# One stage of a fused RWKV and mixture-of-experts kernel: narrower loads of k, other places for the routing's work

## The chip, the cores and the metric

The kernel runs on one core of a Trainium2 chip. The metric is the device time of one execution in microseconds (us). Three runs of the kernel before gave 303.65, 304.31 and 305.09 us; the median is 304.31 us. A separate execution was profiled; it took 301.18 us.

The core has five engines, each with its own in-order queue: PE (TensorE) multiplies matrices into PSUM, DVE (VectorE), ACT (ScalarE) and POOL (GpSimd) work on tiles, and SP issues nearly all the DMAs. An instruction that waits holds everything behind it on its engine.

## The reference

Attention part, for 4 batches, 8 heads, 768 tokens and a head dimension of 48:

```
for t in range(768):
    cur     = einsum('bhd,bhe->bhde', u * k[t], v[t])
    y[:, :, t] = einsum('bhd,bhde->bhe', r[t], state + cur)
    state   = w[t][..., None] * state + einsum('bhd,bhe->bhde', k[t], v[t])
```

Its output is laid out as 3072 tokens of 384 values, x, which go through a mixture of 8 experts (hidden width 1024) with a skip test:

```
compute = x @ w_skip > 0            # the other tokens are copied
e       = argmax(x @ w_gate)        # one expert for each token
out     = x + softmax_weight[e] * (relu(x @ w1[e]) @ w2[e])
```

## The kernel before, in words

The first half of the program is the attention part, the second half the experts. The attention is cut into 24 chunks of 128 tokens: 4 batches of 6 chunks, the state starting from zero in each batch. A loop `for s in range(-2, n + 1)` writes the work out by hand in a software pipeline; the order in which it is written is the order of every engine's queue. In step s it

- issues the loads of chunk s+4 (three buffers `wrk`; each holds w, r and k side by side in 1545 words for each row) and of v,
- prepares chunk s+2: `prep_scan` (DVE: scan q over w; POOL: rk = r*k for the bonus), `prep_keys` (DVE: L290 takes 1/q at the chunk's first token, L292 multiplies it by `rowsk`, which is one in the 96 rows in use and zero in the others, and puts it into the word ahead of w; POOL: kq = k*q), `prep_reads` (DVE: scan rh over w and that word; POOL: rp = r*rh),
- works on chunk s+1: `scores` (PE, from kq and rp), `rows_of_keys` (PE transposes kq, ACT copies it to kt), two `mask`s (DVE), `bonus_sums` (PE, into psY) and `bonus` (DVE multiplies psY by v),
- finishes chunk s: `update` and `carry` (PE adds kt*v to the state, ACT scales it and copies it to sblk), `outputs` (PE adds masked scores times v, and state times rp, to psY), `evict` (ACT copies psY to xT) and `rows_out` (PE turns xT back into rows and makes the gate logits).

psY is one buffer: `bonus_sums(s+1)` writes it only after ACT's copy xT of chunk s. A `wrk` buffer of 128 rows holds 96 rows in use (16 to 111); the 16 rows on each side are loaded from the neighbouring chunks in the same DMA and are finite but meaningless; `rowsk` makes what depends on them zero.

Every 6 chunks a `router` runs over the logits. It is a generator; `drip()` at fixed places in the step runs it on by one or two pieces, so its small DVE instructions fall between those of the chunks. What it wants done on PE or ACT it puts into the list `held`, which `flush()` empties at two places in the step, and it goes on only when the list is empty. `ranks` are eight short products of which DVE needs the result (`pss`); `places` are the products with one-hot rows (`hot`), which put token numbers into a table. One-hot rows are made by `mark`, two for each step, by two ACT operations each (`dd`, then `hot`); eight of 24 are made by DVE. After the third group, `early()` (L525) multiplies a count `ohs` by ones on PE (L528, psC), and starts a gather of the first expert's tokens, for which PE waits at the end of the attention.

In 12 of the steps a slice of an expert's weights is split in two parts for exactness: ACT casts the upper part (L89), and POOL subtracts it from the raw weights for the lower part (L90), at the end of the step.

Of the kernel before, what the change touches and what calls it, by code (L numbers as in the profile page):

```python
# [21 lines left out]
P = 128  # L22
# [34 lines left out]
def rwkv_moe_kernel(ctx, tc, wrk, wrk0, vN, uP, wgs, wgp, w12, cst, out):  # L57
# [40 lines left out]

    def drain(g):
        for _ in g:  # L100
            pass
# [20 lines left out]
    with tc.tile_pool(name="att", bufs=2) as att, \  # L122
# [22 lines left out]
        def load_chunk(i):  # L145
            b, c = seq[i]
            rows = wrk.rearrange("b c g d n -> (b c g d) n")
            at = 2 * D * i
            t = wrk_sb[i % NBUF]
            vt = vt_sb[i % (NBUF + 1)]  # L150
            if i == 0:
                nc.sync.dma_start(t[KO:LO, :R_OFF], rows[:2 * D, :R_OFF])
                nc.sync.dma_start(t[KO:LO, R_OFF:V_OFF], rows[:2 * D, R_OFF:V_OFF])
                nc.scalar.dma_start(c_sb[:, :C_IOTA], cst[:, :C_IOTA])
                shifted(nc.scalar, u_sb, uP)
                for g in range(2):
                    load_vt(nc.scalar, vt, i, g)
                return
            if i < n - 1:
                nc.sync.dma_start(t, rows[at - KO:at - KO + P, :V_OFF])  # L160
            else:
                nc.sync.dma_start(t[KO:LO], rows[at:at + 2 * D, :V_OFF])
            for o in range(2):
                load_vt(nc.sync, vt, i, o)
# [46 lines left out]
        hd = scratch(NP).rearrange("p (a o) -> p a o", o=1)  # L211
# [8 lines left out]
        def clear_rk(eng, i):  # L220
            eng.memset(wrk_sb[i][:, R_OFF:], 0.0)

        def setup():
# [4 lines left out]
            nc.vector.memset(warm, 0.0)  # L228
            nc.gpsimd.memset(vt_sb[1], 0.0)
            load_chunk(1)  # L230
            load_v(0)
            nc.vector.memset(pss, 0.0)
# [4 lines left out]
            nc.vector.tensor_reduce(rowsk, ident[:, KO:LO], axis=AX, op=ALU.add)  # L237
            nc.scalar.activation(junk0, warm[:, 0:1], AF.Exp)
            for z in psa:
                nc.scalar.copy(z.rearrange("p a j -> p (a j)"), warm)  # L240
            nc.gpsimd.memset(vt_sb[2], 0.0)
# [44 lines left out]
        def prep_keys(i):  # L286
            wk = work[i]
            heads = wk["w"][:, 0:NP * CW].rearrange("p (a j) -> p a j", a=NP)
            at = heads[:, :, 0:1]
            nc.vector.reciprocal(hd if i > 0 else at, wk["q"][:, :, 0:1])  # L290
            if i > 0:
                nc.vector.tensor_scalar(at, hd, rowsk, None, op0=ALU.mult)  # L292
            kq = wk["kq"] = att.tile([P, NP, P], F32, tag="kq", name=f"kq{i}")
            nc.gpsimd.tensor_tensor(kq, wk["k"], wk["q"][:, :, 1:1 + P], op=ALU.mult)  # L294
# [111 lines left out]
        def router(i0, m):  # L406
# [67 lines left out]
            def mark(c):  # L474
                dd = att.tile([P, 2 * P], BF16, tag="dd", name=f"dd{i0}_{c}")
                hot = att.tile([P, 2 * P], BF16, tag="hot", name=f"hot{i0}_{c}", bufs=NC)
                nc.scalar.activation(dd, iota, AF.Square, bias=r1[:, c], scale=-1.0)
                nc.scalar.activation(hot, dd, AF.Relu, bias=rows1_, scale=-2.0)
                hots[c] = hot
# [107 lines left out]
        with tc.manual_schedule():  # L587
            setup()
            fill(FILL0)
            for s in range(-2, n + 1):  # L590
# [16 lines left out]
                if s == LATE:  # L607
                    nc.sync.dma_start(wgs_sb, wgs)
                if on(s - 1):
# [15 lines left out]
                flush()  # L625
                if on(s + 2):
                    prep_keys(s + 2)
                    drip(pace[0])
                    if s != -1:
                        prep_reads(s + 2)  # L630
                if s == -2:
# [7 lines left out]
                if on(s + 1):  # L639
                    scores(s + 1)  # L640
                    rows_of_keys(s + 1)
                    drip(2 * pace[0])
# [3 lines left out]
                    bonus_sums(s + 1)  # L646
# [23 lines left out]
                if 3 <= k < 9:  # L670
                    split_slice(0, 3 + k, nc.gpsimd)
                if 12 <= k < 18:
                    split_slice(1, k - 12, nc.gpsimd)
# [349 lines left out]
```

## Time and profile before

| what | value |
|---|---|
| median of three runs | 304.31 us |
| the profiled execution | 301.18 us |
| its span, first to last instruction | 299.4 us |
| PE busy | 275.0 us, 92% of the span |
| DVE busy | 223.8 us, 75% |
| ACT busy | 168.1 us, 56% |
| POOL busy | 138.6 us, 46% |
| DMA, mean | 216 GB/s, 64.62 MB |

The shares are means over two stages. In the attention (about the first 149 us) PE, DVE, ACT and POOL all work, each waiting for the others; in the experts PE is busy without a gap. In the timeline an instruction's duration can overlap the next one's start on PE, so the distance between starts is what a piece of work costs there. "Idle before" and the bracket behind a row name what ended the engine's wait.

### The profile page before, as it was taken

To read this page: it belongs to the slowest core of one execution; us is meant where nothing else is said; L and a number is where in the kernel's file an instruction comes from. 1 tells how busy PE (TensorE), PEld (TensorE's weight loads), DVE (VectorE), ACT (ScalarE), POOL (GpSimd) and SP (SyncE) were. 2 spreads that over 40 slices of the span, in tenths; PEclk is the share of its full clock that TensorE was granted. 3 is DMA by queue.
4 is the path that set the end of the run, shared out by engine and by line. 5 is a ranking of instruction groups with operands and counts; after the bars stand their busy time and mean duration, and the time that the engine had idled before them with its cause. 6 is when DMAs were issued, how large, how long until landed. Compare 5 with 4: busy or idle time off the path is not lost.

```text
span 299.4 us, 8963 instructions
## 1 busy us (share of the span) xinstructions
PE 275.0 (92%) x3581; PEld 247.8 (83%) x3581; DVE 223.8 (75%) x434; ACT 168.1 (56%) x470; POOL 138.6 (46%) x136
## 2 busy tenths in 40 slices
PE   6697998998889979879999999999999999999993
PEld 2476877777767867768798999999999999999993
DVE  7869999898989988986373788784958859496320
ACT  3265645779565986587432485581837649183310
POOL 4867765969975689776115761402011020201101
PEclk9999999999999999999999999999999999999999
DMA  7979999996799968865604798866265663620001
GB/s 217 246 198 311 349 352 371 309 303 194 240 332 297 333 187 285 219 210 180 209 28 114 231 373 308 274 207 234 71 231 208 210 251 129 237 107 26 9 2 41
DMA packets 26548, 64.62 MB, mean 216 GB/s; under 512 B 4886, under 2 KB 15930, under 8 KB 26496
## 3 DMA queue, kind: packets, MB, share of 16 engines
q1 hardware_dynamic: 23904, 58.14, 59.4%
q0 software_dynamic: 2048, 5.48, 5.5%
q8 instruction: 30, 0.49, 0.7%
q10 hardware_dynamic: 544, 0.33, 0.6%
q14 instruction: 22, 0.18, 0.2%
HBM read 56.88 MB, written 7.86 MB: 216 GB/s over the span
## 4 chain that ended last, share of the span: by engine, by line
issue 32%; PE 12%; DVE 7%; DMA 7%; POOL 6%; ACT 5%; POOLq 1%; SPq 0%; DVEq 0%
POOL out L745 5%; DMA r<-w 4%; PE psY L378 2%; PE psH L115 2%; PE psA L326 2%; PE psX L394 2%; DMA vt<-wrk 2%; PE psY L382 1%; DMA xg<-out,idr 1%; PE psY L345 1%; DVE w2l L90 1%; DVE psY L349 1%; DVE asb L332 1%; ACT xT L387 1%; PE psT L316 1%
## 5 line engine op out<-in xcount | busy, mean ns | idle before, releaser
L745 POOL DMA_INDIRECT out<-fin,ids x16 | 16.9, 1058 | 101.1 <-DVE fin L840 93.3
L814 ACT ACTIVATE hh<-psH 128x256 fp32r<-128x256 f32 x60 | 23.1, 384 | 55.2 <-PE psH L809 52.1
L809 PE MATMUL psH<-xTh,w1l 128*128 128x256 f32 x168 | 47.5, 283 | 0.0
L808 PE MATMUL psH<-xTl,w1h 128*128 128x256 f32 x168 | 47.5, 283 | 0.0
L807 PE MATMUL psH<-xTh,w1h 128*128 128x256 f32 x168 | 47.5, 283 | 0.0
L831 PE MATMUL psO<-w2h,hh 128*128 128x384 f32 x120 | 40.9, 341 | 0.0
L833 PE MATMUL psO<-w2h,hl 128*128 128x384 f32 x120 | 40.2, 335 | 0.0
L832 PE MATMUL psO<-w2l,hh 128*128 128x384 f32 x120 | 40.1, 334 | 0.0
L819 DVE SCALAR_TENSOR_TENSOR hl<-psH,hh 128x256 fp32r<-128x256 f32 x60 | 25.2, 420 | 12.3 <-ACT hh L814 12.0
L378 PE MATMUL psY<-asb,v 128*48 128x128 f32 x384 | 26.5, 276 | 8.4 <-DVE psY L349 8.4
L304 POOL TENSOR_TENSOR rp<-wrk,rh 128x512 f32<-128x512 f32 x23 | 27.2, 1182 | 12.5 <-DVE rh L299 7.6
L283 POOL TENSOR_TENSOR rk<-wrk 128x512 f32<-128x512 f32 x24 | 31.3, 1304 | 3.6 <-DMA wrk<-wrk 3.6
L332 DVE TENSOR_TENSOR asb<-psA,c_sb 128x512 f32<-128x512 f32 x48 | 30.5, 677 | 3.0 <-PE psA L326 2.8
L274 DVE TENSOR_TENSOR_SCAN q<-wrk,pss 128x520 f32<-128x520 f32 x24 | 29.3, 1222 | 4.5 <-DMA wrk<-wrk 4.4
L294 POOL TENSOR_TENSOR kq<-wrk,q 128x512 f32<-128x512 f32 x24 | 28.3, 1180 | 8.6 <-DVE q L274 4.7
L809 PEld LDWEIGHTS psH<-xTh,w1l 128*128 128x128 f32 x168 | 32.2, 192 | 0.0
L808 PEld LDWEIGHTS psH<-xTl,w1h 128*128 128x128 f32 x168 | 32.2, 192 | 0.0
L807 PEld LDWEIGHTS psH<-xTh,w1h 128*128 128x128 f32 x168 | 32.2, 191 | 0.0
L299 DVE TENSOR_TENSOR_SCAN rh<-wrk,pss 128x520 f32<-128x520 f32 x24 | 29.7, 1236 | 1.7
L89 ACT CAST w2h<-r 128x512 fp32r<-128x512 f32 x48 | 27.9, 625 | 2.0 <-DMA r<-w 2.0
L90 DVE TENSOR_TENSOR w2l<-r,w2h 128x512 fp32r<-128x512 f32 x42 | 27.8, 687 | 1.5 <-ACT w2h L89 0.5
L378 PEld LDWEIGHTS psY<-asb,v 128*48 128x48 f32 x384 | 20.4, 123 | 10.0 <-DVE psY L349 9.8
(149 smaller groups left out, 594.3 us busy)
## 6 DMA issues: line engine op xcount, KB each, us to landing
r<-w SPq DMA_DIRECT2D x48, 512.0 KB, 5.3
wrk<-wrk SPq DMA_DIRECT2D x22, 772.5 KB, 5.8
v<-vN SPq DMA_DIRECT2D x24, 192.0 KB, 5.2
out<-x SPq DMA_DIRECT2D x24, 192.0 KB, 4.6
vt<-wrk SPq DMA_DIRECT2D x46, 96.0 KB, 5.3
wrk<-wrk SPq DMA_DIRECT2D x1, 579.4 KB, 4.8
wrk<-wrk SPq DMA_DIRECT2D x1, 384.0 KB, 4.4
out<-fin,ids POOLq DMA_INDIRECT x16, 3.9
```

The costliest lines, as they stand in the source:

```text
L90: (eng or nc.vector).tensor_tensor(dst_l, src, dst_h.bitcast(F32), op=ALU.subtract)
L283: nc.gpsimd.tensor_tensor(work[i]["rk"].rearrange("p a j -> p (a j)"), t[:, R_OFF:K_OFF], t[:, K_OFF:V_OFF], op=ALU.mult)
L299: nc.vector.tensor_tensor_scan(rh.rearrange("p a j -> p (a j)"), wk["w"][:, 0:NP * CW], ones_at[:, :NP * CW], 1.0, op0=ALU.mult, op1=ALU.max)
L332: nc.vector.tensor_tensor(s, psa[g], tri.rearrange("p (o j) -> p o j", o=1).to_broadcast([P, NP, P]), op=ALU.mult)
L378: nc.tensor.matmul(y_at(a, g), v[:, 2 * a + g], wk["asb"][g][:, a], start=False, stop=True, skip_group_check=True)
L745: sc = nc.gpsimd.indirect_dma_start(out=out, out_offset=bass.IndirectOffsetOnAxis(ap=ids[:, s % 2, s // 2:s // 2 + 1], axis=0), in_=o, in_ ...
L807: nc.tensor.matmul(ps, w1h[:, o:o + P], xTh[:, kc], start=(kc == 0), stop=False)
L808: nc.tensor.matmul(ps, w1h[:, o:o + P], xTl[:, kc], start=False, stop=False)
L809: nc.tensor.matmul(ps, w1l[:, o:o + P], xTh[:, kc], start=False, stop=(kc == KC - 1))
L831: nc.tensor.matmul(pso, h[j, fc][0], w2h[:, o], start=(fc == 0), stop=False)
L832: nc.tensor.matmul(pso, h[j, fc][0], w2l[:, o], start=False, stop=False)
L833: nc.tensor.matmul(pso, h[j, fc][1], w2h[:, o], start=False, stop=(fc == FC - 1))
```

## The change

Five edits, all in the attention part.

1. w and r are loaded by 128 rows as before, k by its 96 rows in a DMA of its own. The rows of k beside them are cleared once for each of the three buffers at the start (POOL), so every product with k is zero there. L292, the scratch word `hd` and the making of `rowsk` at the start go; the reciprocal writes straight into `wrk`. `rowsk`, which a test at the end still uses, is loaded by three small DMAs in step 18.
2. `mark` makes a one-hot row by one POOL instruction in place of two on ACT.
3. The lower part of a weight slice (POOL) is written one step later, behind the next step's rp; ACT's cast stays.
4. The first `flush()` of a step moves from behind `outputs(s)` to behind `rows_of_keys(s+1)`.
5. `bonus_sums(s+1)` moves from behind the masks to directly behind `scores(s+1)`, ahead of the transposes.

The core of the diff:

```diff
+    def split_high(e, i):
...
+        nc.scalar.copy(hi, raw)
+        low_parts.append(lambda: nc.gpsimd.tensor_tensor(lo, raw, hi.bitcast(F32),
+                                                         op=ALU.subtract))
...
-            if i < n - 1:
-                nc.sync.dma_start(t, rows[at - KO:at - KO + P, :V_OFF])
-            else:
-                nc.sync.dma_start(t[KO:LO], rows[at:at + 2 * D, :V_OFF])
-            for o in range(2):
-                load_vt(nc.sync, vt, i, o)
+            to, at_ = (t[:, :K_OFF], at - KO) if i < n - 1 else (t[KO:LO, :K_OFF], at)
+            nc.sync.dma_start(to, rows[at_:at_ + to.shape[0], :K_OFF])
+            nc.sync.dma_start(t[KO:LO, K_OFF:], rows[at:at + 2 * D, K_OFF:V_OFF])
+            if i > 1:
+                for o in range(2):
+                    load_vt(nc.sync, vt, i, o)
...
-            eng.memset(wrk_sb[i][:, R_OFF:], 0.0)
+            eng.memset(wrk_sb[i][:, R_OFF if i == 0 else K_OFF:], 0.0)
...
+            clear_rk(nc.gpsimd, 1)
+            load_chunk(1)
             nc.gpsimd.memset(vt_sb[1], 0.0)
-            load_chunk(1)
             load_v(0)
+            for o in range(2):
+                load_vt(nc.sync, vt_sb[1], 1, o)
...
-            nc.vector.tensor_reduce(rowsk, ident[:, KO:LO], axis=AX, op=ALU.add)
...
+            clear_rk(nc.gpsimd, 2)
             nc.gpsimd.memset(vt_sb[2], 0.0)
...
-            at = heads[:, :, 0:1]
-            nc.vector.reciprocal(hd if i > 0 else at, wk["q"][:, :, 0:1])
-            if i > 0:
-                nc.vector.tensor_scalar(at, hd, rowsk, None, op0=ALU.mult)
+            nc.vector.reciprocal(heads[:, :, 0:1], wk["q"][:, :, 0:1])
...
             def mark(c):
-                dd = att.tile([P, 2 * P], BF16, tag="dd", name=f"dd{i0}_{c}")
                 hot = att.tile([P, 2 * P], BF16, tag="hot", name=f"hot{i0}_{c}", bufs=NC)
-                nc.scalar.activation(dd, iota, AF.Square, bias=r1[:, c], scale=-1.0)
-                nc.scalar.activation(hot, dd, AF.Relu, bias=rows1_, scale=-2.0)
+                nc.gpsimd.tensor_scalar(hot, iota, r1[:, c], None, op0=ALU.is_equal)
...
                 if s == LATE:
                     nc.sync.dma_start(wgs_sb, wgs)
+                    shifted(nc.sync, rowsk, cst[:, C_HS + 2:C_HS + 3])
...
                     outputs(s)
-                flush()
                 if on(s + 2):
                     prep_keys(s + 2)
                     drip(pace[0])
                     if s != -1:
                         prep_reads(s + 2)
+                while low_parts:
+                    low_parts.pop()()
...
                     scores(s + 1)
+                    bonus_sums(s + 1)
                     rows_of_keys(s + 1)
+                    flush()
                     drip(2 * pace[0])
                     mask(s + 1, 0)
                     mask(s + 1, 1)
                     drip(pace[0])
-                    bonus_sums(s + 1)
                     bonus(s + 1)
...
                 if 3 <= k < 9:
-                    split_slice(0, 3 + k, nc.gpsimd)
+                    split_high(0, 3 + k)
                 if 12 <= k < 18:
-                    split_slice(1, k - 12, nc.gpsimd)
+                    split_high(1, k - 12)
```

Three places show how the queues change. Line numbers of the new kernel are higher by 10 to 18 for the same instruction, and a scan is named SCALAR_TENSOR_TENSOR here.

DVE at the ranks of the first group, before; `oh` is what the ranks need, `pss<-ex` (the sum of the exponentials) lies in the PSUM bank that they write, `asb` are the masks:

```order
L274 SCALAR_TENSOR_TENSOR q_922<-wrk_86,pss 128x520
L432 TENSOR_TENSOR oh_926<-key,pss 128x48
L290 RECIPROCAL pss<-q_922 128x4
L292 TENSOR_SCALAR wrk_86<-pss,rowsk 128x4
L447 TENSOR_REDUCE pss<-ex_840 128x6
L299 SCALAR_TENSOR_TENSOR rh_956<-wrk_86,pss 128x520
L449 TENSOR_SCALAR pss<-pss 128x6
L452 RECIPROCAL gall<-pss 128x6
L332 TENSOR_TENSOR asb_8_988<-psA_111,c_sb 128x512
L332 TENSOR_TENSOR asb_8_990<-psA_112,c_sb 128x512
```

DVE at the same place in the changed kernel:

```order
L288 SCALAR_TENSOR_TENSOR q_925<-wrk_86,pss 128x520
L443 TENSOR_TENSOR oh_929<-key,pss 128x48
L303 RECIPROCAL wrk_86<-q_925 128x4
L310 SCALAR_TENSOR_TENSOR rh_950<-wrk_86,pss 128x520
L458 TENSOR_REDUCE pss<-ex_843 128x6
L460 TENSOR_SCALAR pss<-pss 128x6
L343 TENSOR_TENSOR asb_8_997<-psA_111,c_sb 128x512
L343 TENSOR_TENSOR asb_8_999<-psA_112,c_sb 128x512
```

L292 is gone, and the two small instructions on `pss` that stood around the scan rh now both stand between rh and the masks.

PE at the same place, before, from the last product of `outputs` (state times rp) to the ranks, which the scores of chunk 8 follow:

```order
L382 MATMUL psY<-rp_750,sblk_114 48x128 x8
L435 LDWEIGHTS trib
L435 MATMUL pss<-oh_926,trib 128x48
L437 LDWEIGHTS onesb
L437 MATMUL pss<-ohs,onesb 128x48
L440 LDWEIGHTS onesb
L440 MATMUL pss<-oh_926,onesb 128x40
```

PE there in the changed kernel, from the last product of the scores:

```order
L337 MATMUL psA_112<-rp_846,kq_840 64x64
L356 MATMUL psY<-rk_826,ubk_sb 48x128 x8
L327 MATMUL psT_981<-c_sb,kq_840 128x128 x4
L446 LDWEIGHTS trib
L446 MATMUL pss<-oh_929,trib 128x48
L448 LDWEIGHTS onesb
L448 MATMUL pss<-ohs,onesb 128x48
L451 LDWEIGHTS onesb
L451 MATMUL pss<-oh_929,onesb 128x40
L451 LDWEIGHTS onesb
```

The ranks stand behind the scores, the bonus sums (`psY<-rk`) and the transposes (`psT`) of chunk 8, no longer ahead of them.

POOL at the end of the third group, before, from the rp of chunk 22 to the first gather; `ohs` is what PE's psC needs:

```order
L304 TENSOR_TENSOR rp_2341<-wrk_87,rh_2339 128x512
L90 TENSOR_TENSOR w1l_1_1856<-r_10_1527,w1h_1_1855 128x512
L283 TENSOR_TENSOR rk_2418<-wrk_88 128x512
L294 TENSOR_TENSOR kq_2454<-wrk_88,q_2416 128x512
L521 TENSOR_TENSOR ohs<-ohs,os_2456 128x8
L304 TENSOR_TENSOR rp_2461<-wrk_88,rh_2459 128x512
L536 DMA xg_65<-out,id_71 128x384
```

POOL in the changed kernel, from the same rp:

```order
L315 TENSOR_TENSOR rp_2317<-wrk_87,rh_2315 128x512
L108 TENSOR_TENSOR w1l_1_1839<-r_10_1518,w1h_1_1838 128x512
L487 TENSOR_SCALAR hot_2_2360<-iota,rall 128x256
L487 TENSOR_SCALAR hot_3_2362<-iota,rall 128x256
L297 TENSOR_TENSOR rk_2390<-wrk_88 128x512
L305 TENSOR_TENSOR kq_2411<-wrk_88,q_2388 128x512
L315 TENSOR_TENSOR rp_2415<-wrk_88,rh_2413 128x512
L108 TENSOR_TENSOR w1l_1_1839<-r_10_1518,w1h_1_1838 128x512
L530 TENSOR_TENSOR ohs<-ohs,os_2465 128x8
L545 DMA xg_65<-out,id_71 128x384
```

Two one-hot rows stand ahead of rk, and rp and a lower part of weights stand ahead of `ohs`.

## Rows read from the trace of the kernel before

**Rows 1.** Timeline of PE, one whole step (start us, duration us, engine, line, operation)
```profile
33.00 1.05 PE L326 MATMUL psA<-rp,kq 64*64 64x128 f32 x32
33.98 0.66 PE L316 MATMUL psT<-c_sb,kq 128*128 128x128 f32 x4
34.57 0.65 PE L345 MATMUL psY<-rk,ubk_sb 64*48 64x128 f32 x16
35.15 1.14 PE L394 MATMUL psX<-wgp_sb,xT 128*128 128x105 f32 x8
36.72 1.04 PE L378 MATMUL psY<-asb,v 128*48 128x128 f32 x15
37.69 0.65 PE L382 MATMUL psY<-rp,sblk 64*48 64x128 f32 x16
38.16 1.05 PE L326 MATMUL psA<-rp,kq 64*64 64x128 f32 x32
```

**Rows 2.** Timeline of DVE over the same step, some rows
```profile
31.19 1.23 DVE L274 TENSOR_TENSOR_SCAN q<-wrk,pss 128x520 f32<-128x520 f32 x1
32.45 0.19 DVE L290 RECIPROCAL pss<-q 128x4 f32<-128x4 f32 x1
32.67 0.22 DVE L292 TENSOR_SCALAR wrk<-pss,rowsk 128x4 f32<-128x4 f32 x1
33.01 1.24 DVE L299 TENSOR_TENSOR_SCAN rh<-wrk,pss 128x520 f32<-128x520 f32 x1
...
35.95 1.23 DVE L274 TENSOR_TENSOR_SCAN q<-wrk,pss 128x520 f32<-128x520 f32 x1
```

**Rows 3.** Timeline of DVE, chunk 0, the only one without L292
```profile
5.36 0.18 DVE L290 RECIPROCAL wrk<-q 128x4 f32<-128x4 f32 x1
5.57 1.24 DVE L299 TENSOR_TENSOR_SCAN rh<-wrk,pss 128x520 f32<-128x520 f32 x1
```

**Rows 4.** Waits, 8 to 205 us: waiting line, releaser, total us, times, longest
```profile
PE psY L378 <- DVE psY L349: 8.4, 10, 1.8
PE psY L345 <- ACT xT L387: 3.5, 5, 1.0
DVE pss L290 <- PE pss L511: 2.5, 3, 1.4
DVE pss L290 <- PE pss L440: 1.6, 2, 0.8
```

**Rows 5.** Groups by line, 0 to 215 us (count | busy us, mean ns | idle before)
```profile
L294 POOL TENSOR_TENSOR kq<-wrk,q 128x512 f32<-128x512 f32 x24 | 28.3, 1180 | 8.6 <-DVE q L274 4.7 <-DMA wrk<-wrk 3.9
L90 POOL TENSOR_TENSOR w2l<-r,w2h 128x512 fp32r<-128x512 f32 x6 | 7.6, 1274 | 4.4 <-ACT lgs L401 3.1 <-ACT w2h L89 1.2
L633 POOL MEMSET vt<- 128x512 f32 x1 | 0.5, 525 | 0.0
L477 ACT ACTIVATE dd<-iota,rall 128x256 bf16<-128x256 bf16 x16 | 8.1, 503 | 0.0
```

**Rows 6.** Timeline: scores of chunks 3 and 11; product of `early`
```profile
27.83 1.05 PE L326 MATMUL psA<-rp,kq 64*64 64x128 f32 x32
71.25 1.05 PE L326 MATMUL psA<-rp,kq 64*64 64x128 f32 x32
141.03 0.16 PE L528 MATMUL psC<-ohs,onesb 128*1 128x1 bf16 x1
```

**Rows 7.** Timeline of ACT over the step of rows 1
```profile
34.67 0.59 ACT L318 COPY kt<-psT 128x512 f32<-128x512 f32 x1 [0.81 <-PE psT L316]
37.00 1.20 ACT L368 ACTIVATE psu<-psu,q 128x48 f32<-128x48 f32 x4
38.44 0.59 ACT L387 COPY xT<-psY 128x512 f32<-128x512 f32 x1
```

**Rows 8.** Timeline of DVE: the scan of chunk 3
```profile
21.45 1.24 DVE L274 TENSOR_TENSOR_SCAN q<-wrk,pss 128x520 f32<-128x520 f32 x1 [2.72 <-DMA wrk<-wrk]
```

**Rows 9.** The page, DMA issues (count, KB each, us to landing)
```profile
wrk<-wrk SPq DMA_DIRECT2D x22, 772.5 KB, 5.8
```

More of the change, by code (lines that the diff above doesn't have):

```diff
@@ L97, in split_slice @@
         split(wsp[e, 2 * q][:, cs], wsp[e, 2 * q + 1][:, cs], raws[e, q][:, cs], eng)
+    low_parts = []
+    def split_high(e, i):
+        q, cs = i // 6, slice((i % 6) * 512, (i % 6 + 1) * 512)
+        for k in (2 * q, 2 * q + 1):
+            if (e, k) not in wsp:
+                wtile(e, k)
+        hi, lo, raw = wsp[e, 2 * q][:, cs], wsp[e, 2 * q + 1][:, cs], raws[e, q][:, cs]
+        nc.scalar.copy(hi, raw)
+        low_parts.append(lambda: nc.gpsimd.tensor_tensor(lo, raw, hi.bitcast(F32),
+                                                         op=ALU.subtract))
     def drain(g):
@@ L210, in rwkv_moe_kernel @@
         ones_at = ones_w.bitcast(U8)
-        hd = scratch(NP).rearrange("p (a o) -> p a o", o=1)
         iotaw = scratch(P)
```

## The prediction

> **What bounds the kernel now.** I read the page's shares first: PE 92%, DVE 75%. They average two stages, so next the timeline of the attention. In a step in which nothing extra happens, PE works without a gap from scores to scores, 33.00 to 38.16, 5.16 us [rows 1]. By starts: scores 0.98, transposes 0.59, bonus sums 0.58, psX and psu 1.57, masked scores times v 0.97, state times rp 0.47. DVE needs 4.76 for the same step (31.19 to 35.95) [rows 2], so it has 0.4 to spare, and PE is the bound. The extra steps differ: the waits of PE are for DVE's `bonus` (8.4 us in 10 waits) and for ACT's copy xT (3.5 in 5) [rows 4]. The first are steps with routing work on DVE, the second steps with one-hot rows on ACT. So the change can win only there and at the start; in the ordinary steps it can win nothing and may lose. The experts' stage is PE alone and moves as a whole. I work in three stretches: to the scores of chunk 3 (27.83), from there to those of chunk 11 (71.25), and on to psC (141.03) [rows 6]. Behind psC stands the gather for which PE waits, so what comes after keeps its length.
>
> **L292.** From reciprocal to scan it is 0.22 + 0.34 us [rows 2]; in chunk 0, without L292, the scan starts 0.21 after the reciprocal [rows 3]. Each of 23 chunks saves 0.35 on DVE, 8.0 in all. In an ordinary step that is worth nothing, since PE hides it. It counts where DVE is late: about two steps per router, and one more with `sg`.
>
> **The reciprocal and pss.** Writing to `wrk`, the reciprocal no longer waits for PE's work in pss: 0.8 for the ranks and about 0.8 for the places, twice or three times [rows 4]. What is late next is the sum of exponentials, which writes pss too. It now stands between rh and the masks, behind ranks that stand behind the scores, the sums and the transposes. DVE's masks could start when the scores end; now they wait 0.58 + 0.59 for sums and transposes, about 0.3 for eight short products (estimated from four transposes' 0.59), and two small DVE operations of about 0.2 each (the reciprocal's row): 1.9 us. Behind the masks stand `bonus` and with it PE's next product. Behind the ranks PE has psX and psu (1.57) [rows 1] to do before it needs `bonus`; I count 0.6 of the 1.9 as hidden by that. For the pair of routing steps I get: saved 0.7 (L292 twice), 0.8 (the ranks' wait) and 0.3 (one small operation and a hop), given back 1.3: a gain of 0.5 a router.
>
> **One-hot rows.** ACT loses two operations of about 0.5 a row (L477, and L478 like it) [rows 5], 2 us in each of 8 steps. The wait for xT, 3.5 us [rows 4], falls mostly in these. On POOL no row shows this operation. Nearest from below: a memset writes 128x512 in 0.525, so 256 words take about 0.3. From above: a product of two inputs takes 1.18 for 512, so 0.6 for 256 by rate [rows 5], and 1.18 if size did not matter. I take 0.45, between the first two, since there is one input and one output. A step with a weight slice then holds three products and a lower part, 3 x 1.2 + 1.27 = 4.9, plus 0.9: 5.8 against 5.16. POOL falls behind by 0.6 in each of three such steps; rp is ready over 3 us ahead of its scores, so PE does not feel it, up to about 0.7 us per row.
>
> The Trainium skill ("GPSIMD Engine Reference", section 4.1, Engine selection) puts one-input work on this engine at roughly line rate, which would make it the 0.3 of the memset; no row here shows it for a comparison. By that the wait at psC below would be 0.6 shorter.
>
> **Lower parts a step later.** POOL's waits of 3.1 and 1.2 us for ACT ahead of w2l [rows 5] go, worth nothing to PE, since POOL had slack. The price is at the end: behind rp of chunk 22 POOL now does a lower part, two one-hot rows, rk, kq, rp, another lower part and `ohs`: 1.27 + 0.9 + 3 x 1.2 + 1.27 + 0.2 = 7.2 us. I put the end of that rp 3.2 into the step of chunk 21, and PE at psC 4.2 into the next, 6.2 later. PE waits about 1.1 at psC, with the first expert's gather behind it. Before, `ohs` stood ahead of rp and was early.
>
> **Sums behind the scores.** The sums need xT. With the transposes ahead, 0.59 us of PE work covered a late xT; now nothing does. In the ordinary step xT is copied from 38.44 to 39.03, scores end at 39.14 [rows 1, 7]: in time by 0.1. But kt is now copied 0.6 later, since the transposes come after the sums, and ACT goes on from there: kt 0.59, ends and lows about 0.2, a cast of about 0.6 (shape of kt), logits and x about 0.55, carry to xT 1.44 (37.00 to 38.44) [rows 7], xT 0.59, then PE's sums and transposes 1.17: with hops 5.5 us around. Where a weight slice is cast this ring is longer than 5.16 by 0.35 to 0.4; without it 4.9, which fits. Most cast steps are DVE's anyway; it shows in the two steps before chunk 11, 0.8, and 0.2 from small casts in the first steps.
>
> **Loads.** 516.5 + 192 KB in place of 772.5 [rows 9] (by the diff's sizes), 8% less, and the scan q needs only the first. Chunk 3's scan waited 2.72 for its DMA [rows 8]. The load takes 5.8 to land [rows 9]; a third less to wait for might bring it 1 us sooner, one more DMA on SP per chunk ahead of it costs about 0.4 each, with two ahead. I take 0.45 sooner, plus 0.35 for L292: 0.8 at 27.83, between 0.2 and 1.5. The two extra memsets (0.5 each) [rows 5] come before POOL's first product, which waits for its data. Later loads are issued about two steps ahead; the three small ones for `rowsk` stand on SP in step 18 and delay one load by about 1.5, under that cover.
>
> **The sum.** To 27.83: 0.8 gained. To 71.25: 0.5 (first router), 0.6 (one wait for xT), less 0.8 and 0.2: 0.1, say 0.2. To 141.03: around chunks 11 to 15 DVE is the chain, from the masks of 11 over `sg` and the second router; it loses 3 x 0.35, 0.55 for places and 0.25 behind ACT, less what the ranks give back, 0.6: 1.2. In the last stretch DVE saves 4 x 0.35 = 1.4 and the wait for xT, its late `bonus` and the places save 1.6 in the step of chunk 21; 0.1 is lost on the way and 1.1 at psC: 1.8. Together 0.8 + 0.2 + 1.2 + 1.8 = 4.0 us. The profiled execution of 301.18 would take 297.2; its span 299.4 would be 295.4. The median shown is 304.31, 3.1 above that execution, and the forecast is for such a median: 300.3.
>
> **Rivals.**
> - *POOL becomes the bound (slower).* If a one-hot row costs the whole 1.18 of kq's row, six steps take 7.3 on POOL against 5.16. The wait at psC grows by 4 us for each us of the row, the first group's stall by 6 from 0.7 on, the second's by 6 from 1.0. At 1.0 that is 2.2 + 1.8, and the gain is gone: this is the point from which it decides. At 1.18 it is 2.9 + 2.9 + 1.1 = 6.9, so 307.2. For it: no row shows the operation, and bf16 with a scalar for each row is not float32. Against: by rate even the two-input row gives only 0.6.
> - *ACT's ring binds every step (no change).* If the hops are longer than I think, some ten full steps lose 0.4: gain 0, 304.3. For it: xT is in time by 0.1 only. Against: the casts are in half of the steps, many hidden behind DVE.
> - *More of the waits go (faster still).* If half of the 8.4 us behind `bonus` goes and the start gains 1.5, with no wait at psC: 8 us, 296.3. For it: DVE loses 8.0 in all. Against: the ranks' new wait.
> - *A first-call cost.* One stop of 6 us on POOL at the first one-hot row would leave 1.6 of it in slack and put 4.4 on PE: 304.7. Against it: 24 kq average 1.18 like any one of them [rows 5], and one such call among them would show as a mean 0.25 higher. The Trainium skill ("GPSIMD Engine Reference", section 2.1, Instruction dispatch) states about 6 us for the first call to a freshly loaded kernel; whether a comparison needs a load no run here shows.
>
> **How the numbers follow.** Forecast 0.54, faster still 0.15, ring 0.15, POOL 0.12, first call 0.04. About 0.5%, 1.5 us, is what a measurement of this kernel can tell from no change. Faster by more: 0.50 of the forecast, 0.15, and half of the ring's, 0.07: 0.72. Slower by more: 0.10 of POOL's and 0.02 of the others. The rest, 0.16, is no change. The forecast's own range, with the row between 0.3 and 0.6 and the start between its bounds, is 298.0 to 302.5. The range that should hold 8 in 10 goes to the faster case and to the ring: 296.0 to 304.0.
>
> **What would show it.** In the changed profile: scan rh 0.2 after the reciprocal; a POOL row for the one-hot of 0.3 to 0.6; no waits of PE for xT near 1 us in the steps with one-hot rows, but ones of some 0.4 in cast steps; DVE's sum of exponentials waiting for PE by over 1 us in two places; PE's psC waiting for POOL's `ohs` by about 1 us; scores of chunk 3 at 27.0, chunk 11 at 70.3, psC at 137.0. The forecast is wrong if the one-hot row takes over 0.7, or if steps without casts get longer than 5.2.

## The result, and the profile after

The changed kernel takes 306.4 us in the median of 20 runs (303.3 to 310.5); the kernel before, run beside it, 303.6. The ratio is 1.008 (95%: 1.005 to 1.011): slower by 0.8%, where 1.3% faster was forecast. The ratios, here and below, leave out executions more than 1.5% above the fastest of their kernel: six of these 20, and in e17 two of 380.5 and 903.5 us. The time lies above the range of 296 to 304. The profiled execution took 307.25 us with a span of 305.5; one execution can lie 4 us off the median, so I use the two traces for what waits for what, and ratios for what it costs.

First the groups by line of the changed kernel, 0 to 215 us, that answer to [rows 5]:

```profile
L305 POOL TENSOR_TENSOR kq<-wrk,q 128x512 f32<-128x512 f32 x24 | 28.4, 1182 | 6.0 <-DVE rnk L472 2.9 <-DMA wrk<-wrk 2.4 <-DVE q L288 0.7
L487 POOL TENSOR_SCALAR hot<-iota,rall 128x256 bf16<-128x256 bf16 x16 | 15.1, 955 | 0.0
L108 POOL TENSOR_TENSOR w2l<-r,w2h 128x512 fp32r<-128x512 f32 x6 | 7.7, 1281 | 0.0
```

The second line is the operation that no row of before showed: 0.955 us a row in the mean, 15.1 in all, twice the 0.45 that I took and just under the point of 1.0 from which the POOL rival decides. The third line has lost its wait for ACT, as forecast.

The waits, 8 to 205 us, that answer to [rows 4]:

```profile
POOL rk L297 <- DMA wrk<-wrk: 13.4, 9, 3.4
PE psY L389 <- DVE psY L360: 9.0, 10, 1.8
DVE pss L458 <- PE pss L451: 4.3, 3, 2.7
PE psA L337 <- POOL rp L315: 2.9, 4, 1.3
PE psY L356 <- ACT xT L398: 2.1, 3, 0.9
PE psC L537 <- POOL ohs L530: 2.1, 1, 2.1
```

PE's waits for `bonus` are no shorter (9.0 for 8.4); two are new, for POOL: rp, 2.9 us in 4 where before had one of 1.3 at the start, and `ohs`, 2.1. The chain that ended last (start, us, what) shows the engine that had been off it:

```profile
110.62 1.13 POOL rp L315
111.75 1.23 POOL w1l L108
112.98 1.90 POOL hot L487 x2
...
116.16 1.18 POOL kq L305
117.34 1.14 POOL rp L315
118.48 1.24 POOL w1l L108
...
136.20 1.84 POOL hot L487 x2
...
141.55 1.22 POOL w1l L108
```

From 110 to 143 us the chain hardly leaves POOL. Before, the same stretch ran over PE, DVE and ACT in turn.

The starts that answer to [rows 6], from PE's timeline:

```profile
28.24 1.05 PE L337 MATMUL psA<-rp,kq 64*64 64x128 f32 x32
...
72.22 1.03 PE L337 MATMUL psA<-rp,kq 64*64 64x128 f32 x31
...
142.98 0.16 PE L537 MATMUL psC<-ohs,onesb 128*1 128x1 bf16 x1 [2.06 <-POOL ohs L530]
```

Forecast were 27.0, 70.3 and 137.0. Of the 6.1 us between the two spans, 1.95 have come up by psC, 1.26 lie between psC and the first expert's product, and 2.9 behind that product, in the experts' stage, where the change moves no work. That last stretch takes 150.4 us in the trace of before and 153.3 here, and 150.3 to 153.7 in the traces of the experiments, so I do not put these 2.9 down to the change.

Last, the granted clock. Windows of the changed kernel (start:end, length, busy us of PE, PEld, DVE, ACT and POOL, then PEclk, DMA share, GB/s):

```profile
10.00:14.00 4.00, 1.23 (x26) 0.99 (x26) 3.75 (x6) 0.59 (x1) 2.40 (x2) 1.00 0.84 249
15.00:21.00 6.00, 5.06 (x59) 4.70 (x60) 4.33 (x6) 2.54 (x9) 4.39 (x4) 0.50 0.50 132
...
86.00:89.00 3.00, 1.44 (x24) 1.21 (x23) 2.23 (x6) 2.76 (x11) 3.00 (x4) 1.00 0.88 277
90.00:93.00 3.00, 3.00 (x56) 2.64 (x56) 1.69 (x4) 0.59 (x1) 3.00 (x3) 0.51 0.64 180
...
141.00:143.00 2.00, 0.02 (x1) 0.00 (x0) 0.00 (x0) 1.42 (x5) 1.93 (x3) 1.00 0.02 4
144.00:148.00 4.00, 4.00 (x71) 3.57 (x68) 1.07 (x2) 0.59 (x1) 1.19 (x1) 0.57 0.90 303
```

The first window of each pair is one in which PE mostly waited (1.23 of 4 us busy, 1.44 of 3, 0.02 of 2). In the second it works without much of a gap, but at 0.50 to 0.57, so for the most part at the lower level, 1.2 GHz in place of 2.4. The profiled execution of before has no such stretch in the attention, though PE was not busy all the time there either:

```profile
10.00:14.00 4.00, 2.41 (x49) 1.76 (x48) 3.89 (x8) 0.65 (x2) 2.52 (x6) 1.00 1.02 297
14.00:18.00 4.00, 2.78 (x55) 2.11 (x56) 3.90 (x6) 2.82 (x11) 4.00 (x4) 1.00 0.40 57
```

### The profile page after: what moved, and what is told of

The parts are those of the page before. It is cut to its first block, busy times and chain, and to the rows that moved or that the text cites. A ratio compares the mean times of both kernels' runs of the same rounds, so it can differ in the third digit from the quotient of the medians.

```text
span 305.5 us, 8979 instructions
## 1 busy us (share of the span) xinstructions
PE 275.9 (90%) x3581; PEld 252.8 (83%) x3581; DVE 217.8 (71%) x410; ACT 152.7 (50%) x438; POOL 154.5 (51%) x154
## 4 chain that ended last, share of the span: by engine, by line
issue 35%; DMA 21%; POOL 18%; PE 14%; DVE 6%; SPq 2%; ACT 2%; POOLq 1%; ACTq 1%; DVEq 0%
DMA wrk<-wrk 15%; POOL out L757 5%; POOL rp L315 3%; POOL kq L305 3%; POOL hot L487 2%; PE psY L389 2%; DMA u_sb<-uP 2%; PE psH L127 2%; POOL rk L297 2%; POOL w1l L108 2%; PE psA L337 2%; PE psY L393 1%; PE psX L405 1%; DMA vt<-wrk 1%; PE psY L356 1%
## 5 line engine op out<-in xcount | busy, mean ns | idle before, releaser
L757 POOL DMA_INDIRECT out<-fin,ids x16 | 17.8, 1110 | 99.6 <-DVE fin L852 93.8
L297 POOL TENSOR_TENSOR rk<-wrk 128x512 f32<-128x512 f32 x24 | 31.1, 1296 | 13.9 <-DMA wrk<-wrk 13.4
L389 PE MATMUL psY<-asb,v 128*48 128x128 f32 x384 | 27.2, 280 | 9.1 <-DVE psY L360 9.0
L337 PE MATMUL psA<-rp,kq 64*64 64x128 f32 (+1 forms) x768 | 27.9, 266 | 2.9 <-POOL rp L315 2.9
## 6 DMA issues: line engine op xcount, KB each, us to landing
wrk<-wrk SPq DMA_DIRECT2D x22, 516.5 KB
```

The costliest lines, as they stand in the source:

```text
L297: nc.gpsimd.tensor_tensor(work[i]["rk"].rearrange("p a j -> p (a j)"), t[:, R_OFF:K_OFF], t[:, K_OFF:V_OFF], op=ALU.mult)
L337: nc.tensor.matmul(psa[g][j:j + HP, a, j:], wk["kq"][rows, a, j:j + HP], wk["rp"][rows, a, j:], start=True, stop=True)
L389: nc.tensor.matmul(y_at(a, g), v[:, 2 * a + g], wk["asb"][g][:, a], start=False, stop=True, skip_group_check=True)
L757: sc = nc.gpsimd.indirect_dma_start(out=out, out_offset=bass.IndirectOffsetOnAxis(ap=ids[:, s % 2, s // 2:s // 2 + 1], axis=0), in_=o, in_ ...
```

## The experiments

The letters in the expectations stand for: A, GpSimd's rows are the loss; B, the later place of the routing's products; C, the load of its own for k; D, the moved sums; K, the granted clock behind PE's waits. Ratios are to the kernel before, run beside each on the same chip, with 95% intervals. The time of before differed by some 2 us from chip to chip, so only ratios are compared.

### One part of the change undone (e1 to e4)

e1, `mark` as before:

```diff
-                nc.gpsimd.tensor_scalar(hot, iota, r1[:, c], None, op0=ALU.is_equal)
+                nc.scalar.activation(dd, iota, AF.Square, bias=r1[:, c], scale=-1.0)
+                nc.scalar.activation(hot, dd, AF.Relu, bias=rows1_, scale=-2.0)
```

> The changed kernel, with the one-hot rows back on ACT in two operations each; all else stays changed. Theory A (GpSimd's rows, 0.92 us each where 0.45 was taken, make POOL the late engine in both halves of the attention, and PE's waits for rp and psC bring its granted clock down): POOL's busy time falls by about 16 us, psC no longer waits for ohs by 2 us, the granted clock in 75 to 100 us is back near 1.00, and the time is 1.5 to 2.5% below the changed kernel: 0.985 to 0.993 of the kernel before (299 to 301.5 us). Theory B (the products of the routing behind the scores are the loss: they make ACT's ex and DVE's masks late): the waits of DVE behind ex stay, ACT has more to do, and the time stays 1.005 to 1.012 of before. Theory C (the second load DMA per chunk is the loss): 1.005 to 1.012 as well, with rk still waiting over 10 us for its DMA.

Measured: 1.019 (1.012 to 1.026). No theory had it: with the rows back on ACT the changed kernel becomes slower still. PE no longer waits for `ohs`, as theory A has it, but its wait for xT grows from 2.1 us:

```profile
PE psY L356 <- ACT xT L398: 10.0, 8, 2.0
```

e2, `flush()` behind `outputs(s)`:

```diff
                     outputs(s)
+                flush()
...
                     rows_of_keys(s + 1)
-                    flush()
```

> The changed kernel, with the products and small copies of the routing issued behind the outputs again, ahead of the transposes; one-hot rows stay on GpSimd. Theory A (GpSimd's rows): PE still waits for rp and psC still for ohs, by 2 us; 1.004 to 1.010 of before. Theory B (routing later): DVE's sum of exponentials no longer waits 4.3 us for the ranks, DVE's dsk and km no longer 3 us for ex, and the time falls to 0.995 to 1.000 of before. Theory C (load): 1.005 to 1.010.

Measured: 1.014 (1.009 to 1.020), no faster than the changed kernel's 1.008. B falls.

e3, `load_chunk`, `clear_rk`, `setup` and `prep_keys` as before:

```diff
-            nc.vector.reciprocal(heads[:, :, 0:1], wk["q"][:, :, 0:1])
+            nc.vector.reciprocal(hd if i > 0 else at, wk["q"][:, :, 0:1])
+            if i > 0:
+                nc.vector.tensor_scalar(at, hd, rowsk, None, op0=ALU.mult)
```

> The changed kernel, with w, r and k loaded by one DMA of 128 rows and the masked heads (L292 of before) again, the memsets and the order of the first loads as before; rows on GpSimd and the later routing stay. Theory A: POOL is still late at psC and at the scores behind the routers; DVE gets 0.35 us a chunk back as work; 1.006 to 1.014 of before. Theory B: the same. Theory C (the load of its own for k brings rk 13.4 us of waits in 9 places, makes the first two steps 3 us longer and lets the clock fall at 16 us): rk's waits are back to about 3.6 us in 2, the steps of chunks 1 and 2 take 6.8 and 5.4 us, and the time is 0.997 to 1.002 of before.

Measured: 1.017 (1.011 to 1.022). C falls too, although rk waits 13.4 us for its DMA in the changed kernel and 4.3 here: POOL's late rk is not what PE waits for. L292 is back in e3 as well; e15, below, undoes the load alone.

e4, `bonus_sums(s + 1)` behind the masks again:

```diff
                     scores(s + 1)
-                    bonus_sums(s + 1)
...
+                    bonus_sums(s + 1)
                     bonus(s + 1)
```

> The changed kernel, with the bonus sums behind transposes and masks again. By all three theories a small thing: PE's waits at the sums for xT (2.1 us in 3) go, and of them 0.5 to 1 us of the time; DVE's bonus is issued behind sums that stand later, which may cost the same again where PE runs without a gap. 1.003 to 1.010 of before. If the ring through ACT were the main loss, it would be 0.998 or less.

Measured: 1.001 (0.997 to 1.005). Of the four this alone is faster than the changed kernel, by 0.7%, a little more than expected.

### Sums alone, and the rest with the sums back (e5, e7, e8)

e5 makes the edit of e4 the other way round in the kernel before.

> The kernel before with one part of the change alone: the bonus sums directly behind the scores, ahead of the transposes. Theory D (the moved sums are the loss: PE has nothing to do while it waits for xT, and the two operations of each one-hot row on ACT make xT late): slower, 1.006 to 1.015 of before, PE's waits for xT over 6 us where before has 3.5. Theory A (GpSimd's rows are the loss): 0.998 to 1.003.

Measured: 1.018 (1.014 to 1.022). Its wait for xT, beside 3.5 in [rows 4]:

```profile
PE psY L345 <- ACT xT L387: 11.6, 9, 2.0
```

ACT's timeline of the same kernel, one step with one-hot rows, shows why:

```profile
70.06 0.59 ACT L318 COPY kt<-psT 128x512 f32<-128x512 f32 x1 [1.33 <-PE psT L316]
...
70.73 0.51 ACT L477 ACTIVATE dd<-iota,rall 128x256 bf16<-128x256 bf16 x1
71.28 0.51 ACT L478 ACTIVATE hot<-dd,c_sb 128x256 bf16<-128x256 bf16 x1
71.69 0.49 ACT L477 ACTIVATE dd<-iota,rall 128x256 bf16<-128x256 bf16 x1
72.22 0.51 ACT L478 ACTIVATE hot<-dd,c_sb 128x256 bf16<-128x256 bf16 x1
72.63 0.60 ACT L89 CAST w2h<-r 128x512 fp32r<-128x512 f32 x1
...
75.05 0.59 ACT L387 COPY xT<-psY 128x512 f32<-128x512 f32 x1
```

From kt to xT ACT works through without a gap. kt waits for the transposes, which stand behind the sums, which wait for the xT before: one ring, longer than PE's step wherever rows are marked.

e7 is e4 with the load and the masked heads of before.

> The kernel of the fourth run (sums back) with, in addition, the load by one DMA and the masked heads as before. Theory C (the load of its own for k makes q and rk late while weights load: q waited 3.2 us at 48 us in the fourth run): q and rk wait for DMAs by no more than before, and the time is 0.990 to 0.998 of before. If the load and the masks were a gain, as the third run has it beside the moved sums: 1.005 to 1.010.

Measured: 1.004 (1.001 to 1.008). C's case is out; the difference to e4's 1.001 lies inside the intervals.

e8 is e4 with `mark` of e1, so the change without its rows on GpSimd and without its moved sums.

> The kernel of the fourth run (sums back) with, in addition, the one-hot rows on ACT. Theory A: POOL is never late, psC does not wait for ohs, 0.985 to 0.996 of before. Theory D (ACT and its ring are what binds, the rows on GpSimd are a gain): the ring has slack with the sums behind the transposes, but two operations of 0.5 us a row come back ahead of xT: 1.001 to 1.008.

Measured: 0.979 (0.976 to 0.982), 295.8 us: 2.1% faster than the kernel before and 2.9% faster than the changed one. Its waits:

```profile
PE psY L389 <- DVE psY L360: 5.4, 8, 1.1
PE psY L356 <- ACT xT L398: 2.8, 4, 0.9
PE psA L337 <- POOL rp L315: 1.3, 1, 1.3
```

Theory A is right, but only beside sums at their old place, and the gain is larger than its 0.985 to 0.996. The four ratios belong together:

| | rows on ACT | rows on GpSimd |
|---|---|---|
| sums behind the masks | 0.979 (e8) | 1.001 (e4) |
| sums behind the scores | 1.019 (e1) | 1.008 (the change) |

The sums behind the scores cost 4.1% with the rows on ACT, 0.7% with them on GpSimd. The rows on GpSimd cost 2.2% with the sums at their old place and give 1.1% with the sums moved. Undoing one of the two alone misleads, as e1 did. With rows on ACT and sums behind the scores, e1 (1.019) and e5 (1.018) come out alike, though e1 has all the other edits and e5 none: nothing of the gain that they bring in e8 shows beside this ring.

### PE kept busy in its waits (e6, e9, e14, e16)

e6 and e9 add idle products to the changed kernel; e9's lines:

```diff
                 if on(s):
+                    if s in {0: 4, 7: 6, 8: 2, 13: 6, 14: 2, 19: 2}:
+                        fill({0: 4, 7: 6, 8: 2, 13: 6, 14: 2, 19: 2}[s])
                     outputs(s)
```

> The changed kernel, with products of constants that nobody reads put on PE where it waits: 5 to 14 of 128x256 in bf16, each about 0.11 us, ahead of the outputs in steps 0, 2, 7, 8, 13, 14, 19 and 20, of the scores of chunks 1, 13 and 19, and of psC. They fill at most two thirds of the waits seen there. Theory K (the loss is the granted clock, which falls to its lower level for 4 to 7 us behind PE's long waits, 14 us of the span in the profiled run): the clock stays at 1.00 in two or all of the three places, the mean clock goes from 0.98 to 0.99 or more and the time to 0.985 to 0.998 of before. Theories A and D (the waits themselves are the loss): the products change nothing or cost 0.5 to 1.5 us: 1.005 to 1.014.

Measured: 1.077. It tells nothing of the theory: the products wrote to the bank of `psu`, and the first of each batch waited for ACT's copy out of it, 19.8 us in 10 waits.

> The changed kernel, with products of constants on PE (128x512 in bf16, nobody reads them) where it waits, this time written to a bank for which nothing waits: 2 to 7 ahead of the outputs of steps 0, 7, 8, 13, 14 and 19, of the scores of chunks 1, 13 and 19, and of psC. In the sixth run they waited for ACT, up to 3.4 us, and made what they were to fill. Theory K (a large part of the loss is the granted clock, which falls behind PE's long waits): no low stretch at 14, 89 or 144 us, mean clock 0.99 or more, 0.990 to 1.003 of before. If the waits alone are the loss: 1.005 to 1.013, and the clock as before or the products in the way.

Measured: 0.996 (0.993 to 1.000). Windows of e9, to be laid beside those above:

```profile
10.00:14.00 4.00, 3.27 (x44) 2.15 (x42) 3.41 (x5) 1.56 (x6) 3.49 (x6) 1.00 1.07 270
...
15.00:21.00 6.00, 4.99 (x108) 4.31 (x112) 3.44 (x5) 2.57 (x10) 2.72 (x3) 1.00 0.66 170
```

At 15 to 21 us PE is as busy as in the changed kernel, but at 1.00, and does 108 products where that did 59. No stretch of the attention is at the lower level in this trace. Products that nobody reads can take no work off PE, and yet the changed kernel became 1.2% faster: I put that down to the clock. Not all of it is loss against before, since that kernel pays for the clock as well in most executions: beside e17 its 23 runs had mean granted clocks of 0.98 to 1.00, the five at 0.996 or more took 301.2 to 301.5 us, and the median of all is 302.8. No run fills the waits of before.

e14 does the same to e4, e16 to e8, at their own waits.

> The kernel of the fourth run (sums back, one-hot rows on GpSimd, 1.001 of before), with idle products of 128x512 in bf16 where PE waited: 2, 3, 6, 3 and 2 ahead of the outputs of steps 0, 2, 7, 13 and 19, 4 and 1 ahead of the scores of chunks 1 and 12, and 6 ahead of psC. If the rows' price against the eighth run (2.2%) is the clock for the most part: 0.983 to 0.990 of before, mean clock over 0.99. If it is the waits for POOL and DVE themselves: 0.993 to 1.003, although the clock is up.

Measured: 0.997 (0.994 to 1.001). Against e16 (0.979, below) that leaves 1.8% of the rows' 2.2% to the waits themselves; the 0.4% between lies inside the intervals. Neither trace has a low stretch in the attention, so they can be laid side by side. From its scores to the next chunk's, chunk 12 takes 6.70 us in e14 and 5.00 in e16, chunk 22 takes 8.48 and 5.75. At chunk 12 of e14 PE waits for the places, behind DVE's `sg` and rh; at chunk 22 for `ohs` on POOL, behind six idle products; and behind psC for the first gather, which landed 7.0 us after its issue here and 5.7 in e16:

```profile
78.10 0.60 PE L520 MATMUL pss<-sg,hot 128*128 128x40 bf16 x12 [1.25 <-DVE rh L310]
...
138.56 0.16 PE L538 MATMUL psC<-ohs,onesb 128*1 128x1 bf16 x1 [0.82 <-POOL ohs L530]
...
146.51 0.55 PE L557 MATMUL psX<-c_sb,xg 128*128 128x128 f32 x3 [1.65 <-DMA xg<-out,id]
```

> The kernel of the eighth run, with idle products where PE still waits: 4, 2, 3, 3 and 2 ahead of the outputs of steps 0, 2, 7, 13 and 19, and 4 ahead of the scores of chunk 1. Theory K: the low stretch at 14 us goes, 1 to 2 us less than the eighth run, 0.970 to 0.977 of before. If the clock at the start costs nothing because loads bind there: 0.976 to 0.983.

Measured: 0.979 (0.975 to 0.983), as e8. The low stretch that e8's trace has at 14 to 18 us is gone, the time is not less. e8's own runs say the same: 295.64 us at a granted clock of 1.00, 295.67 at 0.99. There the clock was not what held the start, as the expectation's second case has it.

### What the other parts are worth (e10 to e12, e15, e17, e18)

e10 is e8 with the flush of e2, e11 with the load of e3, e12 with the lower parts in the step of their cast.

> The kernel of the eighth run (sums back, one-hot rows on ACT: 0.979 of before), with the products of the routing issued behind the outputs as before. If their later place is a gain (reciprocal no longer behind them, ACT's ex and casts off the way): 0.983 to 0.990. If it is a loss, as the prediction's price of 1.3 us a router in given-back waits has it against 1.8 saved: 0.974 to 0.979.

Measured: 0.973 (0.968 to 0.979). With 0.979 for e8 this is no difference that can be told. The later flush is not the gain of the first case; whether it costs a little stays open.

> The kernel of the eighth run, with w, r and k in one DMA, masked heads (one more DVE operation of 0.22 us and a hop per chunk) and the first loads and memsets as before. By the prediction's terms these were worth 0.8 us at the start and 0.35 us of DVE in some ten steps, 2 to 3 us in all: 0.984 to 0.991. By theory C (the second DMA costs as much as the masks give): 0.976 to 0.982.

Measured: 0.985 (0.979 to 0.992), as the prediction's terms have it, though the interval touches that of e8.

> The kernel of the eighth run, with the lower parts of the weight slices on GpSimd in the step of their cast, as before. By the prediction worth nothing to PE while POOL has slack: 0.977 to 0.982. If POOL's wait for ACT's cast (3.1 and 1.2 us of before) held rk and kq back: 0.983 to 0.990.

Measured: 0.977 (0.972 to 0.982). No difference to e8.

e15 is e8 with one DMA for w, r and k and heads that stay unmasked:

```diff
-            nc.sync.dma_start(to, rows[at_:at_ + to.shape[0], :K_OFF])
-            nc.sync.dma_start(t[KO:LO, K_OFF:], rows[at:at + 2 * D, K_OFF:V_OFF])
+                nc.sync.dma_start(t, rows[at - KO:at - KO + P, :V_OFF])
```

> The kernel of the eighth run (0.979 of before), with w, r and k loaded by one DMA of 128 rows and the heads still not masked. In rows that belong to the neighbouring chunk k is then not zero, so scores and what follows from them are those of other data; the instructions are the same. If the masked heads carried the gain measured for both (0.8%): 0.973 to 0.981, as the eighth run or better. If the load of its own for k did: 0.984 to 0.990, with q of the first chunks later.

Measured: 0.980 (0.976 to 0.984), as e8: no gain of the load of its own for k shows in the time. By this, what e11 lost lies in the masked heads or in the order of the first loads and memsets, which e11 has as before and e15 does not; e11 and e15 are too close to each other to show it.

> The kernel before with one part of the change alone: k loaded by 96 rows beside w and r, no masked heads, with the first loads and memsets that belong to it. By the prediction's terms (0.8 us at the start, 0.35 us of DVE a chunk in some ten steps where DVE is late, PE's work in pss no longer waited for): 4 us or 1.3% faster, 0.983 to 0.990 of before. If DVE's savings are hidden without the other parts: 0.995 to 1.000.

Measured: 0.990 (0.986 to 0.994): 1.0% of gain, where the first case has 1.3%.

> The kernel before with one part of the change alone: the lower parts of the weight slices on GpSimd a step after their cast. By the prediction worth nothing to PE: 0.997 to 1.003. If POOL's waits for ACT's casts (3.1 and 1.2 us) were on the path to kq and rp: 0.985 to 0.993.

Measured: 0.993 (0.990 to 0.996). The prediction had nothing here; the time is that of the second case. One candidate for the gain is DVE's `sg`, which has two inputs from SBUF. It stands among POOL's products in the timeline of e18:

```profile
75.68 1.28 POOL L295 TENSOR_TENSOR rk<-wrk 128x512 f32<-128x512 f32 x1
...
77.03 0.38 DVE L513 TENSOR_TENSOR sg<-oh,vals 128x240 bf16<-128x240 bf16 x1
...
77.19 1.26 POOL L306 TENSOR_TENSOR kq<-wrk,q 128x512 f32<-128x512 f32 x1 [0.23 <-DVE q L286]
```

and in the kernel before:

```profile
75.75 1.27 POOL L90 TENSOR_TENSOR w2l<-r,w2h 128x512 fp32r<-128x512 f32 x1 [0.22 <-ACT lgs L401]
...
75.89 1.39 DVE L501 TENSOR_TENSOR sg<-oh,vals 128x240 bf16<-128x240 bf16 x1
...
77.34 0.46 PE L511 MATMUL pss<-sg,hot 128*128 128x40 bf16 x12 [0.88 <-DVE sg L501]
```

`sg` takes 0.38 at the gap between two products of POOL and 1.39 when it meets one; then it ends 0.26 behind POOL's end. In before PE waits 0.88 for it there, 1.6 in two places. A lower part that no longer waits for ACT is through before `sg` starts, and in e18 PE no longer waits for `sg`. That this is the whole 0.7% is not shown: PE's wait for `bonus` falls as well, from 8.4 to 6.6, and in e12 `sg` takes 1.40 in two places again without a longer time than e8's.

### The row by itself (e13)

```diff
+                if c % 2:
+                    nc.gpsimd.tensor_scalar(hot, c_sb[:, C_IOTA:C_IOTA + 2 * P], r1[:, c], None,
+                                            op0=ALU.is_equal)
+                else:
+                    for z in (slice(0, P), slice(P, 2 * P)):
+                        nc.gpsimd.tensor_scalar(hot[:, z], iota[:, z], r1[:, c], None,
+                                                op0=ALU.is_equal)
```

> The changed kernel, with the one-hot rows on GpSimd in two forms: the even ones as two comparisons of 128x128 in bf16, the odd ones as one comparison of 128x256 that reads the row numbers in float32 in place of bf16. If the 0.92 us of a row goes by its elements: 0.46 to 0.5 for each half, and 0.9 for the float32 one. If it is a fixed part: 0.8 or more for each half. If bf16 input is what is slow: the float32 one at 0.45 to 0.6. The time is not what this run is for: 305 to 311 us.

```profile
65.48 1.19 POOL L492 TENSOR_SCALAR hot<-iota,rall 128x128 bf16<-128x128 bf16 x2
66.66 0.91 POOL L488 TENSOR_SCALAR hot<-c_sb,rall 128x256 bf16<-128x256 f32 x1
```

One run, 308.3 us. Half a row takes 0.60 (1.19 for two), a whole one 0.91 from float32 as from bf16: between the first two cases. So 128 words more cost 0.32, and by a straight line through the two sizes (an estimate) 0.27 is a fixed part and 2.5 ns the price of a word. kq, which has two inputs, takes 2.3 ns a word with its fixed part in it (1.18 for 512), the memset 1.0.

## Why the prediction was wrong

Right were the sign of the load with L292 (a gain, e17) and of the moved sums (a loss, e5), the place where POOL would bind, and how: psC late behind a lower part, two rows, rk, kq, rp and another lower part. A gain of 4.0 us was forecast and 0.8%, some 2.5 us, were lost. The steps that failed are the price of a one-hot row and, together with it, that of the moved sums; a term for the clock was missing. In the order of their weight:

- **"I take 0.45, between the first two."** The row costs 0.92 to 0.955. This is the largest term. By the prediction's own slopes a row of 0.92 is worth 4 x 0.47 = 1.9 at psC and 6 x 0.22 = 1.3 in the first group: 3.2 of the 4.0 us are gone, and the forecast would have been 303.5. Measured is the price of the rows at 2.2% against rows on ACT (e8 to e4), some 6.7 us, and 1.8% with the waits filled (e16 to e14). The rows do not decide alone: beside the moved sums they are the lesser evil, by 1.1% (e1). The bound from above, "a product by rate, 0.6", was no bound: it leaves out the fixed part. Only the whole kq row was one. Before had a sign of such a part: POOL's `ohs`, of 128x8, takes 0.20.
- **No term for the clock.** "What comes after keeps its length" was wrong behind psC: 7.98 us to the first expert's product before, 9.24 now, since the scores there ran at the lower level; in e9, at 1.00, it is 8.00. The clock is not the only thing that can lengthen it: in e14, also at 1.00, it is 9.21, by the late gather. e9 puts the clock at 1.2% of the changed kernel, some 3.6 us, a part of which before pays as well; it falls partly on the same places as the rows and the sums, so the three do not add up.
- **"Sums behind the scores": 1.0 us lost.** The ring was seen, with its members, and sized for casts alone. Beside one-hot rows on ACT it costs 1.8% (e5), 11.6 us of waits for xT. In the changed kernel the rows are on GpSimd, and the moved sums cost 0.7% (e4), some 2 us; between e9 and e14, filled, there is no difference left to see.
- **"Lower parts a step later: worth nothing to PE."** Alone they give 0.7% (e18), perhaps by `sg`; beside the other edits no difference shows (e12). In the changed kernel POOL has no gap left at `sg`, which takes 2.09 us at 76.49 and 1.68 at 135.26.
- **L292, the reciprocal, the loads.** The scan starts 0.28 behind the reciprocal's start in place of 0.56 [rows 2], so 0.28 a chunk and not 0.35:

```profile
32.65 0.18 DVE L303 RECIPROCAL wrk<-q 128x4 f32<-128x4 f32 x1
32.93 1.24 DVE L310 TENSOR_TENSOR_SCAN rh<-wrk,pss 128x520 f32<-128x520 f32 x1
```

  Alone this part gives 1.0%, 3 us (e17), with scores of chunk 3 at 27.20 in its trace: right in sign and nearly in size. The term "0.45 sooner" for k's own load is not shown by the times (e15). The start can't be priced from one trace: kernels with these loads have the scores of chunk 3 between 26.70 (e9) and 28.24 (the changed kernel).
- **The ranks' wait**, "over 1 us in two places", came (4.3 in 3, up to 2.7), but the gain of 0.5 a router that was forecast for the flush does not show (e10).

Of the rivals, "POOL becomes the bound" was the nearest. It was given 0.12, since the row of kq was scaled down by size. Its 307.2 belongs to a row of 1.18, though; that the time came so near is in part luck, since at 0.92 it had 303.5, and the sums and the clock make up the rest. A first call does not show: the first two rows take 1.84 together.

Two lines of the Trainium skill bear on this. The prediction cited "GPSIMD Engine Reference", section 4.1, which puts elementwise work with one input at roughly line rate, and worked out 0.3 us a row from it: the rows here say 0.92 for a comparison with a number for each row of the tile, and that decides. The same page of the Trainium skill, section 1 (Specifications), says that POOL shares its SBUF interfaces with DVE, and that DVE's operations with two inputs from SBUF contend; the trace agrees, by `sg`, 0.38 and 1.39.

The fastest versions are e8 and e10, 0.979 and 0.973. What stays open: why low stretches come in some executions of a kernel and not in others (the profiled one of before has none), what filling would give before, by which wait the lower parts gain, and how the 0.7% of the moved sums divides into waits and clock.

## What to carry to other kernels

An operation that no row shows is bounded from above by the whole duration of the nearest row on that engine, not by that duration scaled to size; put the sum at both ends before choosing one. Where PE waits in one long piece, look at the clock behind it as well as at the wait, and test what it is worth: 1.2% in e9, nothing in e16. Edits to one ring (here ACT's copies, PE's sums and transposes, and the rows on ACT or elsewhere) are tested in pairs: undoing one alone gave the wrong sign.

## What the runs showed of the hardware

- A POOL comparison of 128x256 in bf16 with a number for each row takes 0.92 us, of 128x128 0.60, from float32 0.91 (e13); ACT makes the same row in two operations of 0.51.
- A DVE operation with two SBUF inputs (`sg`, 128x240) took 0.38 us at a gap between POOL's two-input products (e18, 77.03), 1.39 beside one, ending 0.26 behind it (before, 75.89), and 2.09 beside two back to back (the changed kernel, 76.49).
- Idle products on PE in its waits kept the granted clock at 1.00 and were worth 1.2% of a kernel with some 13 us near the lower level (6, 3 and 4 in the windows of the changed kernel; e9), but nothing where e8 had one such stretch at 14 to 18 us (e16).
- w and r in 516.5 KB took 6.2 to 7.2 us to land (e12, e8), one load of w, r and k in 772.5 KB 5.8 [rows 9] to 7.4 (e15): the executions differ by more than the two forms.
